# A new order for every engine in an attention and token-mixing kernel

## The chip, the core and the metric

The kernel runs on one core of a Trainium2 chip. A core has a matrix engine (TensorE, PE in the profile), a vector engine (VectorE, DVE), a scalar engine (ScalarE, ACT), a general engine (GpSimd, POOL) and a queue engine (SyncE, SP). Each takes its instructions strictly in the order in which the program gives them, and they wait for one another through semaphores. Loads and stores are DMA transfers, issued by SP, ACT or POOL and carried out by 16 DMA engines. The metric is the device time of one execution in microseconds.

## The reference

Inputs are q, k and v of shape (8 batches, 8 heads, 576 positions, 64), 32 packing queries p per head, and three weights. Two attentions stand one behind the other, then a token mixer:

```python
p_packed = sm_attn(p, k, v)            # 32 x 576 scores per head
out = sm_attn(q, p_packed, p_packed)   # 576 x 32 scores per head
x = out.transpose(0, 2, 1, 3).reshape(B, S, H * D)      # (8, 576, 512)
W_tok = scale * einsum('bsd,btd->bst', x @ w_q, x @ w_k)
y = maximum(einsum('bst,btd->bsd', W_tok, x), 0.0) @ w_out
```

The output is (8, 576, 512) in float32. The kernel computes in bf16 with float32 sums.

## The kernel before

All 8 batches are computed one after another with their steps interleaved. The work is written as some forty kinds of steps, each a small function; a string, ORDER (lines 12 to 59), lists every step of every batch, and a loop at the end of the function walks the string and issues the steps. So ORDER alone sets the sequence on every engine. `S1.5=0,1,6,7` is step S1 of batch 5 with PSUM banks 0, 1, 6 and 7; `GE.5@V` is step GE of batch 5 on VectorE (`@A` ScalarE, `@P` POOL). There are 8 PSUM banks, all in one tile, and a bank that is used again must first have been read out. Steps without an engine letter are TensorE's, or DMA issues: `LD.x` loads are issued by POOL unless a letter says otherwise, `ST` stores by SP unless it says POOL or ACT.

The chain of one batch b, in the order of the data:

- `LD.k`, `LD.v`, `LD.q` load the batch with a conversion to bf16 into one of four buffers each. For batches 0 and 7 q comes in halves: `LD.r0` and `LD.r7` (half 0), `LD.q0` and `LD.q7` (half 1). `LD.g0` is half 1 of the first k; its half 0 comes by `LD.H`, float32, and is converted by HC on ScalarE. `LD.E0`, `LD.E1`, `LD.P0` to `LD.P3` load p, `LD.W0`, `LD.W1` and `LD.O` the weights.
- KT (L246) transposes k in 32x32 blocks on VectorE; S1 (L282 for batches 0 and 1, L292 for the others) makes the scores of p; X1 (L300, L303) is their exponential on ScalarE; TE transposes it (VectorE, from batch 2 on). For the first two batches p is laid out by EC, EX and PB, for the others by PX.
- PV (L325) multiplies with v; RC and PP (L329, L333) normalise; PT transposes the packed result, which is key and value of the second attention.
- QV transposes q; S2 (L383) makes the scores of q; X2 (L388) is their exponential; RS, RR and AM (L404, L409, L415) sum the rows, take the reciprocal and multiply. For batch 5, HA on POOL (L398) first adds the halves of the rows. AM's chunk 3 covers four of the five row tiles (128x1024), chunk 2 the fifth (128x256); batches 0, 1 and 7 use chunks 0, 1 (128x512) and 2.
- AT (L424, L429) transposes the weights on TensorE and AE copies them out of PSUM; QK, QKE and QD make the mixer's small weights and a second copy of them; WKQ (L451, L456) and WE make the mixer's projections; GM, GE, Y, YE, MX (L502), MR (L508) mix the tokens; RL, RLF and RLR (L513, L515) are the ReLU.
- OT (L550) multiplies by w_out: five steps per batch, of four 128x512 matmuls each; the fifth (`OT.1.4` and so on) serves two batches at once. OH (L587) are two half-width ones at the very end. OE, OEF and OEH copy the results out of PSUM (L131 on ScalarE, L135 on VectorE); ST, STF and STH store them.

`SET` steps are memsets and other small preparations (`SET.v1` fills the ones in a v buffer, L213; `SET.idb` casts an identity). `WARM.n` issues n matmuls (L622) whose result nobody reads; they fill TensorE's time. `HOLD.v7` is a tiny DMA on SP that reads the last v buffer, so that the stores listed behind it on SP are not issued before v7 has landed. POOL's loads are also bounded by their semaphores: eight of them serve in turn, and a ninth load waits for the first to land.

The loop that does it:

```python
for item in ORDER.split():
    name, _, bk = item.partition("=")
    name, _, eng = name.partition("@")
    ...
    elif f[0] == "WARM":
        ps = bank(int(bk), [512])
        for _ in range(int(f[1])):
            nc.tensor.matmul(ps, warm[:, 0:P], warm, start=True, stop=True)
    else:
        bk = [int(z) for z in bk.split(",")] if bk else None
        steps[f[0]](*[int(z) for z in f[1:]], eng,
```

Of the kernel before, what the change touches and what calls it, by code (L numbers as in the profile page):

```python
# [33 lines left out]
MX.2.0=0,1 PV.4.0=6,7 PV.4.1 RS.3.4@V RL.2.1@A OE.1.0@A RL.2.0@A OT.1.2=4,5 RC.4@V RR.3.4@V PP.4.1@V
PP.4.0@V LD.q5 AM.3.3@P OT.1.3 PT.4@V QV.4.2@V OE.1.1@A QK.4=7 MR.2=0,1 QK.3=6 AM.3.2@V AT.3.3=2
AT.3.2=3 S2.4.2=4,5 AE.3.3@V RLR.2@A QKE.3@A AE.3.2@A QKE.4@A X2.4.2@A S2.4.3=0,1 KT.5.2@V X2.4.3@A
QD.3@P WKQ.3.0=2,3 WKQ.3.2 WKQ.3.1 OT.2.2=4,5 WE.3.2@A RS.4.4@V S1.5=0,1,6,7 GM.3=2 X1.5.1@A OT.2.3
KT.6.2@V GE.3@A X1.5.0@A Y.3=6,7 OT.2.0=2,3 YE.3@A OE.2.1@A MX.3.0=6,7 MX.3.1=0,1 RR.4.4@V TE.5.1@V
TE.5.0@V RL.3.0@A OT.2.1 RL.3.1@V PV.5.0=4,5 OE.2.0@A LD.v6 LD.q6 AM.4.3@P LD.k7 LD.v7 QD.4@P
AM.4.2@V PV.5.1 S1.6=0,1,6,7 RC.5@V AT.4.3=2 AT.4.2=3 PP.5.0@V PP.5.1@V OT.3.0=4,5 X1.6.0@A X1.6.1@A  # L40
AE.4.3@V AE.4.2@V PT.5@V TE.6.0@V QV.5.2@V TE.6.1@V WKQ.4.0=6,7 WKQ.4.1 WKQ.4.2 OT.3.1 QK.5=2
WE.4.2@A OE.3.0@A GM.4=3 GE.4@V MR.3=6,7 S2.5.3=0,1 Y.4=4,5 RLR.3@V YE.4@V QKE.5@A X2.5.3@A
PV.6.0=2,3 LD.r7 LD.q7 ST.0.0@P ST.0.1@P QD.5@P PV.6.1 S2.5.2=4,5 RC.6@V MX.4.1=0,1 PP.6.1@V PP.6.0@V X2.5.2@A
MX.4.0=6,7 OT.3.2=4,5 RL.4.1@A HA.5@P OT.3.3 RL.4.0@A PT.6@V QV.6.2@V RS.5.4@V S2.6.2=0,1 X2.6.2@A
S2.6.3=2,3 MR.4=6,7 RR.5.4@V QK.6=0 X2.6.3@A RLR.4@V OT.3.4=1 AM.5.3@P AM.5.2@P KT.7.2@V OE.3.1@A
# [609 lines left out]
```

## Time and profile before

| | us |
|---|---|
| median of 3 runs | 106.33 (106.15 to 106.53) |
| the profiled execution | 106.69 |
| its span, first to last instruction | 104.9 |
| TensorE busy | 93.5 (89%) |
| VectorE busy | 75.1 (72%) |
| ScalarE busy | 65.8 (63%) |
| POOL busy | 45.9 (44%) |

The span begins with the first instruction of the program. A slice of the page's second part is a fortieth of the span, and a digit is the busy share in tenths. A line of a timeline gives the start, the duration, the engine, the line of the program, the operation, output and input, shapes and count, and in brackets the idle time before it with what ended it. TensorE's matmuls overlap, so the price of a step is read from its start to the next start. A line of DMA issues gives the size and the median time from issue to landing. A line of windows gives the stretch, its length, the busy time with the instructions in brackets, the clock share, the share of the DMA engines and GB/s.

### The profile page before, as it was taken

To read this page: it belongs to the slowest core of one execution; us is meant where nothing else is said; L and a number is where in the kernel's file an instruction comes from. 1 tells how busy PE (TensorE), PEld (TensorE's weight loads), DVE (VectorE), ACT (ScalarE), POOL (GpSimd) and SP (SyncE) were. 2 spreads that over 40 slices of the span, in tenths; PEclk is the share of its full clock that TensorE was granted. 3 is DMA by queue.
4 is the path that set the end of the run, shared out by engine and by line. 5 is a ranking of instruction groups with operands and counts; after the bars stand their busy time and mean duration, and the time that the engine had idled before them with its cause. 6 is when DMAs were issued, how large, how long until landed. Compare 5 with 4: busy or idle time off the path is not lost.

```text
span 104.9 us, 3598 instructions
## 1 busy us (share of the span) xinstructions
PE 93.5 (89%) x1528; PEld 52.2 (50%) x1550; DVE 75.1 (72%) x151; ACT 65.8 (63%) x108; POOL 45.9 (44%) x74
## 2 busy tenths in 40 slices
PE   0994998998998999989999999999999999999930
PEld 0341654564645654655547436565466653743510
DVE  5056069969798889588598988969995989768000
ACT  5140404234657867879989897598996885556640
POOL 5977343554783226222054559635847029000000
PEclk9999999999999999999999999999999999999999
DMA  3999999999999999999999999999999999978693
GB/s 86 239 153 194 211 202 204 211 209 210 206 213 213 204 207 216 210 210 206 212 212 207 216 205 208 213 210 211 212 337 399 409 414 408 391 273 355 243 337 121
DMA packets 14079, 25.16 MB, mean 240 GB/s; under 512 B 2160, under 2 KB 7024, under 8 KB 14064
## 3 DMA queue, kind: packets, MB, share of 16 engines
q0 software_dynamic: 10160, 15.83, 81.4%
q1 hardware_dynamic: 3488, 8.91, 22.0%
q8 instruction: 12, 0.20, 0.7%
q10 hardware_dynamic: 416, 0.20, 0.7%
q14 instruction: 3, 0.02, 0.1%
HBM read 30.28 MB, written 9.44 MB: 379 GB/s over the span
## 4 chain that ended last, share of the span: by engine, by line
PE 67%; DVE 9%; DMA 7%; ACT 5%; issue 4%; POOL 3%; DVEq 0%; POOLq 0%; ACTq 0%
PE ps L550 26%; PE ps L622 8%; DMA k_sb<-in_k_dram 7%; PE ps L325 6%; PE ps L383 5%; PE ps L502 4%; PE ps L429 3%; PE ps L456 3%; PE ps L451 3%; POOL a L415 3%; DVE rs L404 3%; PE ps L282 2%; PE ps L477 2%; PE ps L346 2%; PE ps L292 2%
## 5 line engine op out<-in xcount | busy, mean ns | idle before, releaser
L550 PE MATMUL ps<-wout,relu 128*128 128x512 bf16 x113 | 29.4, 380 | 0.7 <-issue 0.2
L622 PE MATMUL ps<-o 128*128 128x512 bf16 x73 | 20.3, 410 | 2.9 <-DVE o L138 2.4
L415 POOL TENSOR_TENSOR a<-e,rr 128x1024 bf16<-128x1024 f32 (+2 forms) x10 | 12.5, 1263 | 17.3 <-DVE rr L409 17.3
L131 ACT ACTIVATE o<-ps 128x1024 f32<-128x1024 f32 (+2 forms) x18 | 15.2, 857 | 4.7 <-PE ps L550 4.7
L550 PEld LDWEIGHTS <-relu 128*128 128x128 bf16 x124 | 10.8, 98 | 11.9 <-issue 2.2
L388 ACT ACTIVATE e<-ps 128x256 f32<-128x256 f32 (+2 forms) x19 | 11.1, 620 | 7.7 <-PE ps L383 7.5
L622 PEld LDWEIGHTS <-o 128*128 128x128 bf16 x82 | 7.6, 103 | 11.4 <-issue 2.9
L180 POOL DMA_DIRECT2D v_sb<-in_v_dram x16 | 10.1, 637 | 6.9 <-PE ps L508 2.1
L404 DVE TENSOR_REDUCE rs<-e 128x16 f32<-128x512 f32 (+2 forms) x13 | 10.9, 842 | 2.0 <-ACT e L388 1.8
L246 DVE STREAM_TRANSPOSE kT<-k_sb 128x1152 uint32<-128x1152 uint32 (+1 forms) x9 | 11.0, 1228 | 1.6 <-DMA k_sb<-in_k_dram 1.6
L513 ACT ACTIVATE relu<-ps 128x1024 bf16<-128x1024 f32 (+1 forms) x12 | 11.1, 955 | 0.6 <-PE ps L508 0.6
L246 DVE STREAM_TRANSPOSE qT<-q_sb 128x1152 uint32<-128x1152 uint32 (+1 forms) x10 | 11.1, 1106 | 0.0
L131 ACT ACTIVATE wkq<-ps 128x448 bf16<-128x448 f32 (+1 forms) x10 | 7.1, 732 | 2.9 <-PE ps L456 2.2
L303 ACT ACTIVATE e1T<-ps 128x576 bf16<-128x576 f32 x12 | 7.4, 650 | 1.6 <-PE ps L292 1.6
L325 PE MATMUL ps<-v_sb,e 64*64 64x192 bf16 x288 | 7.5, 245 | 0.0
L383 PEld LDWEIGHTS <-qT 64*128 64x128 bf16 x320 | 5.5, 94 | 2.8 <-DVE qT L246 1.6
L300 ACT ACTIVATE e<-ps 128x1152 bf16<-128x1152 f32 x2 | 2.3, 1130 | 7.2 <-PE ps L282 7.2
L456 PE MATMUL ps<-aT,pqk 128*128 128x256 bf16 (+1 forms) x48 | 6.8, 246 | 0.0
L325 PEld LDWEIGHTS <-e 64*64 64x64 bf16 x288 | 5.8, 107 | 1.9 <-ACT e L300 1.0
L383 PE MATMUL ps<-ppT,qT 64*128 64x64 bf16 x320 | 6.4, 190 | 0.3 <-DVE qT L246 0.2
L515 DVE TENSOR_SCALAR relu<-ps 128x1024 bf16<-128x1024 f32 (+1 forms) x6 | 6.0, 1034 | 0.5 <-PE ps L502 0.5
L189 POOL DMA_DIRECT2D q_sb<-in_q_dram x6 | 4.3, 720 | 4.8 <-DMA q_sb<-in_q_dram 2.8
(78 smaller groups left out, 143.0 us busy)
## 6 DMA issues: line engine op xcount, KB each, us to landing
out_dram<-o SPq DMA_DIRECT2D x11, 512.0 KB, 5.9
v_sb<-in_v_dram POOLq DMA_DIRECT2D x16, 288.0 KB, 11.2
k_sb<-in_k_dram POOLq DMA_DIRECT2D x7, 576.0 KB, 11.9
q_sb<-in_q_dram POOLq DMA_DIRECT2D x6, 576.0 KB, 14.3
out_dram<-o SPq DMA_DIRECT2D x5, 256.0 KB, 2.4
q_sb<-in_q_dram POOLq DMA_DIRECT2D x4, 288.0 KB, 11.1
out_dram<-o POOLq DMA_DIRECT2D x2, 512.0 KB, 14.1
out_dram<-orem SPq DMA_DIRECT2D x4, 256.0 KB, 5.8
```

The source lines that it names most:

```text
L131: nc.scalar.activation(o, i, COPY)
L180: nc.gpsimd.dma_start(v_bufs[b % NL][halves(i), 0:7:2], src)
L246: nc.vector.transpose(o, i)
L325: nc.tensor.matmul(T["pv", b][halves(cc), i], lhsT, rhs, start=n == 0, stop=n == R - 1, skip_group_check=True)
L383: nc.tensor.matmul(ps[:, y, t - t0, i], lhsT, rhs, start=e == 0, stop=e == 1)
L388: nc.scalar.activation(e2[:, t0:t1].rearrange("a t (i y n) -> a y (t i) n", i=2, y=2), T["s2", b, c].rearrange("a y t i n -> a y (t i) n") ...
L404: nc.vector.tensor_reduce(rs[:, t0 * H:t1 * H], src, axis=AX, op=ADD)
L415: e.tensor_tensor(a2[:, t0:t1].rearrange("a t i (u l) -> a (t i u) l", l=L), e2v(b, c), T["rr", b][:, t0 * H:t1 * H].to_broadcast((P, (t1 ...
L456: nc.tensor.matmul(o, pqk[:, i, Dl:], aT[:, i, c0:c1], start=i == 0, stop=i == 1)
L513: nc.scalar.activation(o, i, RELU)
L550: nc.tensor.matmul(ps, lhsT, wout[:, j, :], start=j == 0, stop=j == NJ - 1)
L622: nc.tensor.matmul(ps, warm[:, 0:P], warm, start=True, stop=True)
```

## The change

Only ORDER is different; no step's function is touched, and the same steps are issued, apart from the warm-up matmuls (15 groups with 82 matmuls before, 12 groups with 72 after). All engines get another sequence, the PSUM banks are dealt out anew, and 55 steps change engine. Among them:

- memsets v1 and v2 from VectorE to POOL; POOL's loads in another sequence at the start (P1 and P3 early, v0 after q0, k1 later), with QV.0.1 and KT.0.0 ahead of KT.0.1 on VectorE, and PX ahead of QV.1.2 and PT.1
- AM.4.3, AM.5.3, AM.6.3 and AM.7.1 from POOL to VectorE; AM.1.0, AM.2.2, AM.2.3 and AM.4.2 in the main the other way
- QD from POOL to ScalarE (batches 0 and 2) or VectorE (3 to 6); OE.3.0 and OE.6.0 from ScalarE to VectorE; several AE, RL, RLR, GE, YE and WE between the two
- LD.r7 behind HA.5, and LD.q7 behind the store ST.0.0 and behind AM.5.2 on POOL; ST.0.1 later on POOL
- another sequence of the last matmuls, copies and stores

The diff, cut:

```diff
 ORDER = """
-LD.H@S LD.E0@A LD.E1@S SET.v0@V SET.pz0@V SET.aT0@V SET.warm@V SET.tab@A EC@A HC@A EX@V SET.v1@V SET.idf@V PB.0.2@V
-LD.g0 LD.v0 LD.q0 SET.v3@P SET.mask@P PB.0.0@P PB.0.3@V KT.0.1@V KT.0.0@V PB.0.1@V
-WARM.21=1 S1.0=0,2,4 X1.0.0@A WARM.5=7 PV.0.0=0,1 PV.0.1 RC.0@V QV.0.1@V PP.0.0@V PP.0.1@V LD.r0
-LD.k1 LD.W1 LD.W0 SET.aff@P SET.idb@V PT.0@V QV.0.0@V WARM.11=2 S2.0.2=0,1 S2.0.0=2,3 LD.v1 LD.P3
-LD.q1 LD.P2 SET.v2@V KT.1.2@V LD.P1 LD.P0 S2.0.1=4,5 X2.0.1@A X2.0.0@A X2.0.2@A RS.0.1@V SET.aT1@V
...
-PV.6.0=2,3 LD.r7 LD.q7 ST.0.0@P ST.0.1@P QD.5@P PV.6.1 S2.5.2=4,5 RC.6@V MX.4.1=0,1 PP.6.1@V PP.6.0@V X2.5.2@A
-MX.4.0=6,7 OT.3.2=4,5 RL.4.1@A HA.5@P OT.3.3 RL.4.0@A PT.6@V QV.6.2@V RS.5.4@V S2.6.2=0,1 X2.6.2@A
-S2.6.3=2,3 MR.4=6,7 RR.5.4@V QK.6=0 X2.6.3@A RLR.4@V OT.3.4=1 AM.5.3@P AM.5.2@P KT.7.2@V OE.3.1@A
-OT.4.0=2,3 RS.6.4@V S1.7=4,5,6,7 OEF.3.4@A QKE.6@A AT.5.3=1 AT.5.2=0 OT.4.1 AE.5.3@V HOLD.v7
-X1.7.1@A X1.7.0@A AE.5.2@V RR.6.4@V OE.4.0@A WKQ.5.0=4,5 QD.6@P AM.6.3@P AM.6.2@P WKQ.5.2 WKQ.5.1
...
+SET.pz0@V SET.v0@V LD.E0@A LD.H@S LD.E1@S LD.g0 SET.warm@V SET.tab@A SET.idf@V EC@A EX@V PB.0.2@V PB.0.1@V
+SET.aT1@V SET.v2@P LD.P1 LD.q0 HC@A KT.0.0@V LD.P3 PB.0.0@P PB.0.3@V QV.0.1@V KT.0.1@V WARM.31=0 S1.0=0,1,2
+X1.0.0@A LD.v0 WARM.5=3 PV.0.0=4,5 PV.0.1 LD.r0 RC.0@V SET.mask@P PP.0.0@V PP.0.1@V PT.0@V QV.0.0@V LD.W1
+WARM.9=3 S2.0.1=6,7 SET.aff@P SET.idb@V LD.k1 KT.1.2@V S2.0.2=0,1 X2.0.1@A SET.v3@P S2.0.0=2,3 X2.0.0@A
+SET.v1@P LD.W0 RS.0.0@V SET.aT0@V RR.0.0@V LD.P2 LD.v1 AM.0.0@V RS.0.1@V WARM.8=4 S1.1=4,5,6 X1.1.0@A X2.0.2@A
+RS.0.2@V RR.0.2@V AM.0.2@V LD.q1 WARM.5=7 PV.1.0=2,3 QK.0=7 PV.1.1 RC.1@V PP.1.1@V AT.0.0=6 PP.1.0@V LD.P0
+QKE.0@A RR.0.1@V AM.0.1@V PX@V QV.1.2@V AT.0.2=7 AE.0.0@A QD.0@A WARM.2=4 WKQ.0.0=4,5 WARM.1=0 AT.0.1=6
...
+GE.4@V S2.5.2=6,7 X2.5.2@A TE.6.1@V S2.5.3=4,5 TE.6.0@V OE.3.0@V Y.4=0,1 YE.4@V PV.6.0=6,7 PV.6.1 RC.6@V
+PP.6.0@V LD.v7 QK.5=2 X2.5.3@A HA.5@P PP.6.1@V MX.4.1=4,5 MX.4.0=0,1 QKE.5@A QD.5@V RL.4.1@A PT.6@V MR.3=2,3
+LD.r7 RLR.3@A RL.4.0@A OT.3.2=6,7 RS.5.4@V OT.3.3 OE.3.1@A QV.6.2@V OT.3.4=4 MR.4=2,3 ST.0.0@P RLR.4@A
+S2.6.3=0,1 OEF.3.4@A S2.6.2=6,7 RR.5.4@V AM.5.2@P AM.5.3@V OT.4.0=2,3 X2.6.2@A HOLD.v7 AT.5.3=5 KT.7.2@V
+AT.5.2=4 AE.5.2@V LD.q7 ST.3.4 ST.1.4 X2.6.3@A AE.5.3@A ST.2.1 RS.6.4@V RR.6.4@V AM.6.2@P OT.4.1 AM.6.3@V
+OE.4.0@A ST.1.1 S1.7=6,7,0,1 X1.7.0@A TE.7.0@V WKQ.5.0=4,5 WKQ.5.2 WKQ.5.1 WE.5.2@A OT.4.2=2,3 OT.4.3 X1.7.1@A
+TE.7.1@V AT.6.2=6 AE.6.2@A GM.5=7 GE.5@A OE.4.1@A AT.6.3=4 QK.6=5 ST.3.1 QV.7.0@V ST.4.0 Y.5=0,1 AE.6.3@V
+PV.7.0=6,7 PV.7.1 QV.7.1@V YE.5@A MR.5=2,3 RC.7@V QKE.6@A QD.6@V RLR.5@A MX.5.1=0,1 MX.5.0=4,5 PP.7.0@V
+WKQ.6.0=2,3 WKQ.6.1 WKQ.6.2 RL.5.1@A PP.7.1@V OT.5.4=6 PT.7@V S2.7.0=0,1 RL.5.0@A WE.6.2@V S2.7.1=4,5
...
+YE.6@V MX.6.1=6,7 ST.2.0 MX.6.0=2,3 ST.4.1 ST.5.4 AM.7.1@V AT.7.1=4 AM.7.0@P AE.7.2@V QD.7@P AE.7.1@A RL.6.0@A
+AT.7.0=5 OT.5.1 AE.7.0@V ST.3.0 RL.6.1@V WKQ.7.0=4,5 WKQ.7.1 WKQ.7.2 WE.7.0@A OT.6.0=2,3 WE.7.1@V OE.5.0@V
+ST.5.1 ST.5.0 GM.7=6 GE.7@A OT.6.1 OE.6.0@V Y.7=4,5 MR.6=6,7 OT.6.2=0,1 RLR.6@A YE.7@A MR.7=6,7 ST.6.0 RLR.7@V
+MX.7.0=4,5 MX.7.1=2,3 RLF.7.0.0@V RLF.7.0.1@V RLF.7.1.0@V OEF.6.2@A STF.6.2 OT.6.3 OEF.6.3@A STF.6.3
+RLF.7.1.1@A OT.7.4=0 OEF.7.4@V ST.7.4 OT.7.2=6 OEF.7.2@V STF.7.2 OT.7.0=7 OEF.7.0@A OT.7.1=4 OEF.7.1@A
+OH.7.1=5 STF.7.0 STF.7.1 OEH.7.1@V OH.7.0=1 OEH.7.0@A STH.7.1@A STH.7.0
```

## The prediction

> **What bounds the kernel now.** I read the page's slices first, then TensorE's timeline, then the landings of the loads, then VectorE in the stretch where it is fullest.
>
> The slices, 2.62 us each:
>
> ```profile
> PE   0994998998998999989999999999999999999930
> DVE  5056069969798889588598988969995989768000
> DMA  3999999999999999999999999999999999978693
> ```
>
> TensorE is full from about 30 us to 100 us, and the 16 DMA engines are full from 2.6 us to about 92 us. Two resources are nearly used up. VectorE stands at 8 and 9 in slices 21 to 34.
>
> TensorE's timeline, cut to the places the sum uses:
>
> ```profile
> 2.44 6.51 PE L622 MATMUL ps<-o 128*128 128x512 bf16 x21 [2.44 <-DVE o L138]
> 10.35 1.24 PE L282 MATMUL ps<-o,kT 128*64 128x128 bf16 x36 [1.41 <-DVE o L135]
> ...
> 30.67 0.48 PE L292 MATMUL ps<-kT,pT 32*32 32x288 bf16 x32
> ...
> 58.78 0.48 PE L292 MATMUL ps<-kT,pT 32*32 32x288 bf16 x32
> 59.20 0.47 PE L477 MATMUL ps<-wkq,a 128*128 128x64 bf16 x10
> 59.50 1.03 PE L550 MATMUL ps<-wout,relu 128*128 128x512 bf16 x4
> 60.45 0.25 PE L487 MATMUL ps<-pp,g 64*64 64x128 bf16 x4
> ...
> 75.58 0.49 PE L292 MATMUL ps<-kT,pT 32*32 32x288 bf16 x32
> ...
> 84.35 0.78 PE L383 MATMUL ps<-ppT,qT 64*128 64x64 bf16 x40
> ```
>
> The L292 rows are S1.2, S1.5 and S1.7; the last row is S2.7. From start to start each step has a price: S1 0.42, GM 0.30, OT 0.95 (59.50 to 60.45; two in a row 1.78), and likewise WKQ 0.80, PV 0.87, S2 0.70, MX 0.55, AT 0.52, QK 0.36, Y 0.20, MR 0.13. With these, the steps between S1.5 and S1.7 sum to 16.77 against 16.80 measured, and those from S1.7 to S2.7 to 8.78 against 8.77. So TensorE does not wait there; its own work is the bound.
>
> The loads (time to landing; 288 KB each half of q7, 576 KB k7) and VectorE's busy time from KT.5.2 to PT.7:
>
> ```profile
> k_sb<-in_k_dram POOLq DMA_DIRECT2D x1, 576.0 KB, 10.2
> v_sb<-in_v_dram POOLq DMA_DIRECT2D x2, 288.0 KB, 11.7
> q_sb<-in_q_dram POOLq DMA_DIRECT2D x2, 288.0 KB, 13.0
> ```
> ```profile
> 56.80:83.20 26.40, 23.14 (x45) 1.00 1.12 256
> ```
>
> k7 is issued at 63.23 and lands at 73.4; KT.7.2 follows at 73.93 and S1.7 at 75.58. v7 lands at 76.6, r7 at 78.0, q7 (issued 66.00, 13.4) at 79.4. Loads arrive one behind the other, 1.4 us per 288 KB, with 7 to 18 us of queue ahead of each. Both orders load the same bytes before k7, so k7 lands at 73.4 in both unless the queue runs dry.
>
> **The change, part by part.**
>
> Front. QV.0.1 moves ahead of KT.0.1 on VectorE and needs q0. POOL now issues P1 between g0 and q0, and v0 later. By landings (g0 8.6; 0.3 for 64 KB of P, from 24.5, 24.8, 25.1; 1.4 for q0) q0 lands at 10.3 instead of 12.8. QV.0.1 (0.75) and KT.0.1 (0.75) then end at 11.85 and S1.0 starts at 12.1, against 10.35: +1.75. Its 31 warm-ups end near 11.0. Afterwards QV.0.1 (0.75) and the cast idb (0.21) are gone from between RC.0 and QV.0.0, so S2.0 is late by 0.8 to 1.0 only. k1 lands 1.3 later (P1, P3 and W1 are ahead), S1.1 slips by 0.7, PV.1 by 0.6. PX now sits ahead of QV.1.2 and PT.1 and waits for P0 (25.1): S2.1 at about 27.8 against 26.45, while WKQ.0 and GM.0 are done before it. QK.1, Y.0 and S1.2 follow at 29.7 against 30.67. Next v2 decides, loaded behind q2 now: it lands at 33.5 (q2's time before, 22.12 + 11.4), PV.2 runs at 33.7 against 34.51. The delay is covered by warm-ups; without that cover it costs up to 1.75.
>
> Warm-ups: 82 become 72, at 0.216 each when hot (128x512). Behind S1.2 there are 4 instead of 12, 1.7 us less of TensorE work. Between there and S1.5 most of this goes into waiting for loads: S2.3 needs q3 (47.3) plus QV 1.35, S2.4 needs QV.4.2 and PT.4, S1.5 needs k5 (39.49 + 17.1 = 56.6) plus KT.5.2 1.37, so 58.0 against 58.78. What stays: S1.5 0.8 earlier, with OT.2.3 done, MR.2 and QK.4 not.
>
> Small memsets: v1 and v2 move to POOL, 0.64 each by the v3 row against 0.54 on VectorE. They lie beside the load-bound front: nothing. They need only precede PV.1 and PV.2.
>
> Division of the copies. By rows VectorE takes on 2.8 us over the whole (80.8 to 83.6), ScalarE 1.0, and POOL is relieved of 4.1. Between KT.5.2 and PT.7 VectorE's list goes from 25.0 to 27.1: AM.4.3, AM.5.3, AM.6.3 (1.18 each), three QD and OE.3.0 (1.21) come in, against RL.3.1 (1.2), AM.4.2, two RLR, AE.5.3 and others. In measured terms 23.1 busy becomes 25.2 of the same 26.4; the idle 3.3 that absorbed waits shrinks to about 1.2. QD has no VectorE row; bounds are the 32x256 copy (0.22) and POOL's own (0.29); I take 0.22, its kind of instruction. QD on ScalarE (0, 2) takes 0.28 as the 128x128 casts. AE of 128x1024 on ScalarE lies between 0.60 (half the size) and 1.02 (f32): 1.0. WE.6.2 on VectorE lies between 0.62 (half) and 1.21: 1.1.
>
> What this does to TensorE, walked from S1.5 at 58.0 by the prices above: the steps up to S1.7 sum to 17.44 (AT.5 and OT.4.1 now stand ahead of S1.7, QK.6 behind it). MX.3 waits 0.15 for YE.3, which queues behind AM.4.3 and TE.5.1; PV.6 0.25 for v6 and TE.6.0; MX.4 0.4 for YE.4, queued behind OE.3.0. KT.7.2 is queued behind AM.5.3 and starts near 74.7, not at 73.9. S1.7 at 76.4: 0.8 late, with 1.1 us less work ahead of it to S2.7 (7.67 instead of 8.78). That gives 84.1. ScalarE (X2.6, AE.5.3, OE.4.0 ahead of X1.7.0) just serves it.
>
> q7. LD.q7 stood at 66.0 on POOL; now it is behind HA.5, LD.r7, the 512 KB store ST.0.0 and AM.5.2. HA.5 ends near 70.5, RR.5.4 (behind QV.6.2) near 73.4, AM.5.2 (0.61) near 74.1. Then q7's bytes stand behind those of r7 and ST.0.0: 80.7, ST.0.0's own landing before (66.69 + 14.0), is the lower bound; 82.3, that of ST.0.1 beside SP's stores (68.13 + 14.2), the upper. I take 81.0, the nearer in bytes. QV.7.1 then runs to 82.0 ahead of RC.7, QD.6, PP.7, PT.7, which end at 83.2; S2.7 asks for it at 84.1, so 0.9 us cover it. WKQ.6 waits for QD.6 and is just in time.
>
> AM pairs. RR.4.4, RR.5.4 and RR.6.4 now release an AM on VectorE and one on POOL at once. No row before shows two of these side by side: AM.3.3 on POOL (53.59, 1.90) ran beside transposes at their usual 1.34. The bounds are 0 and 0.6 (AM.6.2 waiting out most of AM.6.3, AT.6.2 being next on TensorE); a gain is excluded, since each has its lone price in the sum. I take 0.3, having no nearer row.
> The Trainium skill (SBUF — State Buffer, "SBUF: two separate sides") says that a VectorE operation with two SBUF inputs and a GpSimd operation share one pair of ports, and that whichever starts first holds it throughout. No row of this trace shows it. By that rule the second AM waits out the first; the sum would have 0.6 here instead of 0.3.
>
> Tail. OE.6.0, YE.6, RLF.7.1.0, OEF.7.2 and 7.4 change engine. Walked from S2.7, TensorE's steps take 16.65 to the last OH against 16.3 (84.35 to 100.65): AM.7.1 follows RS.7.1 and YE.6 on VectorE, and WKQ.7 and OT.6.0 wait for AE.7.0 and RL.6.1. After the last matmul, one 0.38 copy and one store, as before. +0.35.
>
> Sum: S2.7 -0.2, AM pair +0.3, tail +0.35: +0.45 on a span of 104.9, so 105.35. The profiled execution took 106.69 in all, 0.36 above the median 106.33; the median stands 1.43 above the span, so **106.8 us**.
>
> **The rivals.** Second, the lead is kept: VectorE's waits turn out smaller than the three I add, S1.7 runs when k7 allows (73.4 + 0.2 + 1.4 = 75.1, or 0.5 before now) with 1.1 less to do: -1.6 at best, with the tail's +0.35 -1.2, halfway 105.5. For it: the fewer warm-ups, S1.5 early. Against: VectorE's 25.2 of 26.4. It decides if KT.7.2 starts before 74.3. Third, q7 arrives after 82, or the AM pairs cost their whole: past 82 every tenth delays PT.7, and past PT.7 at 84.1 also S2.7; at 83 with the pair at 0.6 it is +1.6, 107.9. For it: AM.5.2 stands ahead of LD.q7. Fourth, the steps cancel: 106.3, the change being spent beside the loads.
>
> **How the numbers follow.** Forecast 0.40, lead kept 0.33, late q7 or pairs 0.15, cancelled 0.12. Faster 0.33, within 0.3% (0.32 us, about what measurement of this kernel can tell) 0.13, slower 0.54, from the first (mostly over 0.3%) and the third. The range runs from the better half of the second (105.2) to a little past the third (108.4); the forecast's own is 106.4 to 107.4, by the bounds of pair (0 to 0.6) and q7.
>
> **What would show it.** S1.0 near 12; S1.5 near 58.0; KT.7.2 after 74.5 behind AM.5.3; S1.7 near 76.4 with AT.5 and OT.4.1 before it; q7 landing near 81; VectorE with hardly a gap from 57 to 83; AM on both engines at once, each longer than alone or not; the last matmul near 101.1. I am wrong if S1.5 is already late (then front or queue), or if S1.7 comes at 75 (then VectorE was no bound).

## The result and the profile after

The changed kernel takes 110.41 us (median of 6 runs, 109.37 to 111.26) against 106.39 of the kernel before on the same chip: 1.035 times the time, 95% interval 1.030 to 1.040. It is slower by 4.0 us in the medians and by 3.7 in the ratio, outside the forecast's range. The profiled execution took 110.31 with a span of 108.5. Some executions of this program, in either order, run longer at a lower granted clock; ratios are formed without them, and for two of the experiments too few others were left for a ratio.

The slices of the page of after, 2.71 us each:

```profile
PE   1999999998939979998796999989999899799940
DVE  5075077788898768987699999979999769888610
DMA  3999999999999999999999946999999999999973
GB/s 85 273 180 198 185 201 198 213 212 210 207 214 175 180 187 201 211 205 218 209 213 204 214 86 79 204 211 206 190 248 297 412 411 402 404 402 356 363 287 125
```

TensorE has dents where it had none (slices 12, 15, 20 and 22), and the DMA engines, which were full to 92 us before, fall to 4 and 6 in the 24th and 25th slice: 86 and 79 GB/s in place of some 210.

TensorE's timeline, cut to the same steps and to the four places where it stands longest between S1.2 and S1.7:

```profile
29.08 0.53 PE L288 MATMUL ps<-kT,pT 32*32 32x288 bf16 x32
...
31.89 0.23 PE L420 MATMUL ps<-idb,a 128*128 128x64 bf16 x2 [1.83 <-DVE a L411]
...
40.44 1.04 PE L546 MATMUL ps<-wout,rem 128*128 128x512 bf16 x4 [0.59 <-DVE rem L511]
...
50.90 0.25 PE L483 MATMUL ps<-pp,g 64*64 64x128 bf16 x3
52.19 0.24 PE L483 MATMUL ps<-pp,g 64*64 64x128 bf16 x1 [1.04 <-issue]
...
58.99 0.78 PE L379 MATMUL ps<-ppT,qT 64*128 64x64 bf16 x40 [0.87 <-DVE ppT L242]
61.46 0.48 PE L288 MATMUL ps<-kT,pT 32*32 32x288 bf16 x32
...
79.07 0.48 PE L288 MATMUL ps<-kT,pT 32*32 32x288 bf16 x32
...
87.32 0.78 PE L379 MATMUL ps<-ppT,qT 64*128 64x64 bf16 x40
```

The L288 rows are S1.2, S1.5 and S1.7, the L379 rows S2.4 and S2.7. S1.2 is 1.6 earlier than before, S1.5 2.7 later. Between them lie stops: at AT.1.2 (from 30.05), at OT.1.4, in the middle of Y.2, and ahead of S2.4. The stops of TensorE longer than 0.14 us behind 30 us, measured between its records with the weight loads counted as work, sum to 0.8 before and to 5.6 after: 1.83 at AT.1.2, 0.59 OT.1.4, 1.04 Y.2, 0.68 S2.4, 0.37 PV.6, 0.44 in two places near S2.7, 0.63 at AT.7.1. That is 4.8 more, against 5.3 by which the way from S1.2 to the last matmul grew (69.98 to 75.24). The eight warm-ups that are gone from this way (1.7) are made up in part by matmuls at half clock in one slice (PV.2 took 1.65 instead of 0.94). That slice is not the loss: the profiled executions of e1, e2 and e3 below have a granted clock of 1.00 and take 109.28 to 110.39.

| start, us | before | after | forecast |
|---|---|---|---|
| S1.0 | 10.35 | 10.47 | 12.1 |
| S1.2 | 30.67 | 29.08 | 29.7 |
| S1.5 | 58.78 | 61.46 | 58.0 |
| S1.7 | 75.58 | 79.07 | 76.4 |
| S2.7 | 84.35 | 87.32 | 84.1 |
| end of the last matmul | 100.65 | 104.32 | 101.1 |

The stop at AT.1.2 waits for AM.1.2, the end of a chain on VectorE (sums, reciprocals and multiplication of batch 1). The kernel before has the same step at the same time, with almost no wait:

```profile
31.90 0.23 PE L424 MATMUL ps<-idb,a 128*128 128x64 bf16 x2
```

So TensorE's lead of 1.6 at S1.2 ended here: what it had done ahead, it then waited for VectorE. S1.3 stands at 39.36 after and at 39.25 before. The end of the chain, on VectorE and POOL in the kernel after:

```profile
30.90 0.93 DVE L411 TENSOR_TENSOR a<-e,rr 128x256 bf16<-128x256 f32 x1
```
```profile
30.50 1.04 POOL L411 TENSOR_TENSOR a<-e,rr 128x512 bf16<-128x512 f32 x1 [9.57 <-ACT e1T L299]
```

AM.1.2, 0.42 in the kernel before, took 0.93 beside AM.1.0 on POOL.

The stop ahead of S2.4 waits for PT.4. What stands ahead of PT.4 is the pair AM.3.2 (VectorE, 128x256) and AM.3.3 (POOL, 128x1024). VectorE's and POOL's timelines there:

```profile
55.19 2.01 DVE L411 TENSOR_TENSOR a<-e,rr 128x256 bf16<-128x256 f32 x1
```
```profile
55.01 1.91 POOL L411 TENSOR_TENSOR a<-e,rr 128x1024 bf16<-128x1024 f32 x1 [6.76 <-DVE rec L325]
...
63.44 1.22 POOL L411 TENSOR_TENSOR a<-e,rr 128x256 bf16<-128x256 f32 x1 [5.80 <-ACT e1T L299]
64.61 1.28 POOL L176 DMA_DIRECT2D v_sb<-in_v_dram  x2
```

AM.3.2 takes 0.40 alone; here it ends 0.3 behind POOL's operation. The last two rows are AM.4.2 and, behind it, LD.v6: POOL stood 5.8 us for AM.4.2's turn and issued v6 at 64.6, where the kernel before issued it at 57.2. That is the hole in the DMA row. VectorE's window from 57 to 83 us is as full as forecast (25.2):

```profile
56.80:83.20 26.40, 25.36 (x42) 1.00 1.02 189
```

### The profile page after: what moved, and what is told of

Read it like the earlier page. It is cut to its first block, busy times and chain, and to the rows that moved or that the text cites. A ratio compares the mean times of both kernels' runs of the same rounds, so it can differ in the third digit from the quotient of the medians.

```text
span 108.5 us, 3589 instructions
## 1 busy us (share of the span) xinstructions
PE 95.1 (88%) x1540; PEld 53.3 (49%) x1540; DVE 81.5 (75%) x152; ACT 66.3 (61%) x112; POOL 44.7 (41%) x69
## 4 chain that ended last, share of the span: by engine, by line
PE 41%; DMA 21%; DVE 17%; POOL 9%; issue 5%; ACT 2%; SPq 0%; POOLq 0%; DVEq 0%; ACTq 0%
PE ps L546 17%; DMA k_sb<-in_k_dram 11%; DMA q_sb<-in_q_dram 6%; DVE rs L400 4%; PE ps L321 4%; DVE a L411 4%; DMA o<-in_p_dram 3%; PE ps L379 3%; PE ps L452 3%; DVE qT L242 2%; PE ps L425 2%; POOL v_sb L176 2%; PE ps L447 2%; PE ps L288 2%; PE ps L498 2%
## 5 line engine op out<-in xcount | busy, mean ns | idle before, releaser
L546 PE MATMUL ps<-wout,relu 128*128 128x512 bf16 x124 | 30.5, 380 | 0.0
L411 POOL TENSOR_TENSOR a<-e,rr 128x256 bf16<-128x256 f32 (+2 forms) x9 | 11.4, 1276 | 39.7 <-ACT e1T L299 15.4
L618 PE MATMUL ps<-o 128*128 128x512 bf16 x72 | 19.4, 410 | 2.3 <-DVE o L134 2.3
L127 ACT ACTIVATE o<-ps 128x1024 f32<-128x1024 f32 (+2 forms) x15 | 13.0, 867 | 7.5 <-PE ps L546 7.1
L618 PEld LDWEIGHTS <-o 128*128 128x128 bf16 x72 | 6.7, 103 | 9.8 <-DVE o L134 2.3
L411 DVE TENSOR_TENSOR a<-e,rr 128x512 bf16<-128x512 f32 (+2 forms) x10 | 10.5, 1048 | 0.2
L127 ACT ACTIVATE aT<-ps 128x512 bf16<-128x512 bf16 (+2 forms) x12 | 6.3, 534 | 5.6 <-PE ps L425 4.8
L321 PE MATMUL ps<-v_sb,e 64*64 64x192 bf16 x288 | 9.1, 260 | 0.7 <-issue 0.4
L321 PEld LDWEIGHTS <-e 64*64 64x64 bf16 x288 | 6.9, 114 | 3.0 <-issue 1.2
L379 PE MATMUL ps<-ppT,qT 64*128 64x64 bf16 x320 | 6.4, 190 | 1.1 <-DVE ppT L242 0.9
L379 PEld LDWEIGHTS <-qT 64*128 64x128 bf16 x320 | 5.7, 94 | 2.5 <-DVE qT L242 1.3
L127 ACT ACTIVATE wkq<-ps 128x448 bf16<-128x448 f32 (+1 forms) x8 | 5.8, 731 | 1.7 <-PE ps L447 1.3
```

Source lines behind the costliest of these rows:

```text
L127: nc.scalar.activation(o, i, COPY)
L321: nc.tensor.matmul(T["pv", b][halves(cc), i], lhsT, rhs, start=n == 0, stop=n == R - 1, skip_group_check=True)
L379: nc.tensor.matmul(ps[:, y, t - t0, i], lhsT, rhs, start=e == 0, stop=e == 1)
L411: e.tensor_tensor(a2[:, t0:t1].rearrange("a t i (u l) -> a (t i u) l", l=L), e2v(b, c), T["rr", b][:, t0 * H:t1 * H].to_broadcast((P, (t1 ...
L546: nc.tensor.matmul(ps, lhsT, wout[:, j, :], start=j == 0, stop=j == NJ - 1)
```

## The experiments

Four causes were in question: the late loads on POOL, the AM pairs that hold each other up, the stops with the releaser "issue" (the profile shows nothing that TensorE waits for), and the fuller VectorE. In the diffs a line is a cut of ORDER.

### One cause at a time, taken out of the kernel after

**e1** issues v6 and q6 ahead of the waiting AM.4.2:

```diff
-AM.4.2@P S1.5=2,3,6,7 ... TE.5.1@V LD.v6 OT.2.1 ... LD.q6 RL.3.0@A
+LD.v6 LD.q6 AM.4.2@P S1.5=2,3,6,7 ... TE.5.1@V OT.2.1 ... RL.3.0@A
```

> Changed kernel, with LD.v6 and LD.q6 moved ahead of AM.4.2 on POOL, nothing else. In the changed kernel LD.v6 was issued at 64.6 us, after POOL had waited for RR.4.4 and for the lock, the load queue ran dry around 64 us and k7 landed at 76.6 instead of 73.4. Theory Q (the dry queue is the cause): v6 is issued near 57.7, k7 lands near 73.7, S1.7 comes 2 to 3 us earlier, time about 108. Theory V (VectorE is late before that, S1.5 at 61.5 already): k7 lands near 73.7 as well, but S1.5 stays near 61.5 and S1.7 near 78.9, and only q7's wait near 84 goes: 109.7 to 110.3.

Measured: 109.8 against 106.14, ratio 1.034 (1.026 to 1.043). k7 landed at 73.44 and q7 at 82.27 instead of 76.60 and 84.68, S1.5 came at 60.8, S1.7 at 78.4. The queue no longer runs dry and nothing is gained that a run can tell: TensorE is late at S1.5 already, before any of these loads is needed, as theory V had it.

**e2** puts AM.3.2 ahead of AM.3.3 on POOL, so that no pair stands there:

```diff
-AM.3.2@V
+AM.3.2@P
```

> Changed kernel, with AM.3.2 on POOL ahead of AM.3.3 instead of on VectorE beside it. In the changed kernel AM.3.2 took 2.01 us on VectorE where its form takes 0.41. Theory L (the two engines lock each other out): PP.4.1, QV.4.2 and PT.4 come 1.6 to 2.0 us earlier, S2.4 near 57.2 instead of 59.0, S1.5 near 59.8, and the load of v6 is issued as much earlier; time about 108.6 to 109. Theory Q: v6 is issued earlier by the same 1.6, so a similar gain, but with S1.7 set by k7. If the 2.01 was the operation's own (the line held up by something else), S2.4 stays at 59 and the time at 110.4.

Measured: 109.65, ratio 1.0345 (1.027 to 1.042). The stop ahead of S2.4 is gone, S1.5 comes at 60.8. Yet nothing is gained: the stop in Y.2 grew to 1.39, and PV.6 waits 0.63, here for v6 and at another place of the stream than in the kernel after; all stops together are 6.1 instead of 5.6.

**e3** takes the 128x256 halves of batches 4, 5 and 6 to VectorE, so that they no longer run on POOL beside VectorE's halves:

```diff
-AM.4.2@P ... AM.5.2@P AM.5.3@V ... AM.6.2@P
+AM.4.2@V ... AM.5.2@V AM.5.3@V ... AM.6.2@V
```

> Changed kernel, with AM.4.2, AM.5.2 and AM.6.2 on VectorE, just ahead of or behind AM.b.3 there, so that no AM runs on POOL in these batches. Theory L: each pair costs VectorE 0.41 more and spares POOL's wait of about 1; AM.4.3, 5.3, 6.3 keep 1.2 each; v6 is issued near 57.7, q7 near 74.5; S1.5 stays near 61.5. S1.7 comes only 0 to 0.5 earlier, S2.7 0.5 to 1: time 109.3 to 110. Theory Q: k7 near 73.7 and S1.7 2 to 3 us earlier: about 108.

Measured: 110.42, ratio 1.039 (1.031 to 1.047): nothing gained. On POOL beside VectorE's half they had taken 1.22, 1.56 and 1.58 against 0.61 alone, but TensorE did not wait for them longer than 0.2.

**e4** is e1, e2 and e3 together.

> Changed kernel, with the three edits together: AM.3.2 on POOL, AM.4.2, 5.2, 6.2 on VectorE, LD.v6 and LD.q6 early. Theory L with Q: S1.5 near 59.8, k7 near 73.7, S1.7 near 77, S2.7 near 85: time 107.7 to 108.5; what is still above the kernel before (106.4) is then VectorE's added work and the front. Theory V alone (too much VectorE work, no lock): no more than 0.5 gained.

Measured: 109.98, ratio 1.036 (1.026 to 1.046). S1.5 at 60.5, S1.7 at 78.5. The sum of these three causes is not the loss. Nor is the time a plain sum of stops: those of e4's profile are 4.0 in place of 5.6, and no gain can be told.

### The same causes, put into the kernel before

**f2** moves AM.3.2 ahead of PT.4 in the kernel before, where it stands beside AM.3.3:

```diff
-PT.4@V QV.4.2@V ... QK.3=6 AM.3.2@V AT.3.3=2
+AM.3.2@V PT.4@V QV.4.2@V ... QK.3=6 AT.3.3=2
```

> Kernel before, with one step moved: AM.3.2 on VectorE ahead of PT.4 instead of behind QV.4.2, so that it runs beside AM.3.3 on POOL. Theory L: it takes about 1.8 to 2.0 us instead of 0.39, POOL's AM.3.3 keeps 1.9, and PT.4, QV.4.2 and S2.4 come about 1.6 later than their work asks; time up by 0.4 to 1.2. Rival (the 2.01 belongs to the changed kernel's surroundings): 0.4, time unchanged.

Measured: 107.79 against 106.28, ratio 1.014 (1.007 to 1.022). VectorE, POOL and TensorE in f2:

```profile
53.32 2.00 DVE L415 TENSOR_TENSOR a<-e,rr 128x256 bf16<-128x256 f32 x1
```
```profile
53.13 1.90 POOL L415 TENSOR_TENSOR a<-e,rr 128x1024 bf16<-128x1024 f32 x1 [4.55 <-DVE rr L409]
```
```profile
55.59 0.41 PE L346 MATMUL ps<-wqk,ppT 64*64 64x128 bf16 x8 [1.50 <-DVE ppT L246]
```

POOL started first and kept its 1.90; VectorE's operation, 0.40 alone, ended 0.3 behind it, PT.4 came late and TensorE stood 1.50. This is what the Trainium skill (SBUF — State Buffer, "SBUF: two separate sides") states of the shared pair of ports: whichever starts first holds it for the whole instruction. The pair alone is worth 1.4%.

**f3** holds v6 and q6 behind AM.4.3 in the kernel before:

```diff
-LD.v6 LD.q6 AM.4.3@P
+AM.4.3@P LD.v6 LD.q6
```

> Kernel before, with LD.v6 and LD.q6 behind AM.4.3 on POOL, so that they are issued near 63.3 instead of 57.2 and 58.4. Theory Q: the load queue runs dry near 65, v6, q6 and k7 land 1 to 2 us later, S1.7 follows k7 and the time rises by 1 to 2. Rival (a gap of the queue is hidden by TensorE's backlog): under 0.5.

Measured: 108.66, ratio 1.023 (1.017 to 1.029). Its page shows the same hole in the DMA row, and TensorE's waits a new one that goes back to POOL:

```profile
DMA  2999999999999999999999949999999999999793
```
```profile
PE ps L456 <- POOL pqk L133: 1.4, 1, 1.4
```

QD.4 now has the issue of v6, q6, k7 and v7 ahead of it on POOL in one row, ends at 67.0 and holds WKQ.4 up by 1.4; k7 is late too, and KT.7.2 holds S1.7 up by 0.5. So the edit costs 2.3% where nothing else is late, the larger part of it through QD.4 and only some 0.5 us through the late k7; in the kernel after, where TensorE is late already, issuing the loads early gains nothing that can be told (e1).

### The stops with the releaser "issue"

In the kernel after and in e1 to e4 TensorE stops in Y.2 at the same place of its stream, its 1470th weight load or matmul, and in all of them but e2 again at the 2236th (e2's wait in PV.6, for v6, is at the 2179th). The difference, 766, is three times 256 but for two. The trace's DMA packets have one of 16 KB on the instruction queue 2.2 to 2.6 us before each of these stops ends (in the kernel after at 49.73 and 69.63, for stops that end at 52.19 and 72.05). **f1** takes ten warm-ups away, so that every later instruction stands 20 places further forward:

```diff
-WARM.31=0 S1.0=0,1,2
+WARM.21=0 S1.0=0,1,2
```

> Changed kernel with 21 instead of 31 warm-up matmuls ahead of S1.0, where TensorE waits anyway; all instructions behind them move up by 20 places in TensorE's stream. In all five traces of the changed order TensorE stands still inside Y.2 at the same place of the stream (after 1470 weight loads and matmuls) for 0.66 to 1.39 us, and again inside PV.6 766 instructions later, each time 2.1 to 2.6 us after a 16 KB transfer of the instruction queue began. Theory F (the stall is the fetch of the next 256 instructions): the stall leaves Y.2 and comes 20 instructions later, after OT.1.1 has begun, so it shrinks to 0.3 or less; S1.5 about 0.7 earlier; time 109.3 to 110. Rival (a semaphore of Y.2): the stall stays in Y.2 and the time at 110.2.

Measured: 109.75 against 106.28, ratio 1.032 (1.026 to 1.038). Y.2 has no stop any more; that of PV.6 has moved a few steps on in the order, into the middle of QK.5, and is longer. It is the 2224th instruction recorded in f1, where 19 records are missing:

```profile
70.52 0.30 PE L342 MATMUL ps<-wqk,ppT 64*64 64x128 bf16 x4
72.34 0.30 PE L342 MATMUL ps<-wqk,ppT 64*64 64x128 bf16 x4 [1.52 <-issue]
```

No data, bank or engine decides where TensorE stops, but the count of instructions. By these figures it stops where a block of 256 has been used up before the next one is there. The time of the 256 instructions that end at each stop, without the stop itself: 4.5 us at Y.2 in after (stop 1.04), 4.3 at PV.6 (0.37), 4.6 there in h3 below (0.46). The fastest block of the kernel before takes 5.3 to 5.5 (22 of its records are missing), and none of its stops is of this kind. There is no fixed bound: i2 below stops 0.93 behind a block of 4.9, h4 0.87 behind one of 5.5, while one of 5.2 in i1 passes without a stop. The packet itself begins 2.4 to 4.3 us after TensorE has passed the edge before (46.37 and 49.73 in after, 70.15 and 74.42 in h4); why it varies is not shown. The Trainium skill (Runtime: NRT & Kernel Launch, "Instruction fetch mechanics") has blocks of 16 KiB or 256 instructions, and calls the crossing mostly hidden; the size agrees, the hiding fails here.

**f4** closes what the traces so far named: e4 and f1, OT.1.4 a place later, AM.7.0 on VectorE, and r7 and q7 issued earlier.

```diff
-WARM.31=0 ... OT.1.4=4 OEF.1.4@A X1.3.1@A RS.2.4@V OT.0.2=2,3 OT.0.3
+WARM.21=0 ... X1.3.1@A RS.2.4@V OT.0.2=2,3 OT.1.4=4 OEF.1.4@A OT.0.3
-HA.5@P ... LD.r7 ... LD.q7 ... AM.7.0@P
+LD.r7 LD.q7 HA.5@P ... AM.7.0@V
```

> Changed kernel with every gap of TensorE attacked at once that its trace shows behind S1.3: AM.3.2 on POOL; AM.4.2, 5.2, 6.2 and 7.0 on VectorE; OT.1.4 behind OT.0.2 (it waited 0.6 for RLR.1); 21 warm-ups; LD.v6, LD.q6, LD.r7 and LD.q7 early. Theory S (no single cause; the loss is the sum of TensorE's gaps, 6.0 us in the changed kernel against 2.7 before): gaps fall to about 3 and the time to 107.5 to 108.3. Rival W (too much work on VectorE, so that a closed gap opens elsewhere): gaps stay above 4.5 and the time above 109.

Measured: 110.21, ratio 1.028 (1.017 to 1.040). Theory S missed; the rival's numbers hold (stops of 5.0), but not by its reason: AT.1.2 still waits 1.81, and the stop of QK.5, which has nothing to do with VectorE, is there with 1.38, since f4 has f1's count.

### The division between the engines, and the order

**g1** is the order after with the 55 moved steps back on their old engines, **g2** the order before with the 55 on their new ones. In cut:

```diff
-QD.0@A ... AM.4.3@V ... OE.3.0@V
+QD.0@P ... AM.4.3@P ... OE.3.0@A
```

> The order and the banks after, but each of the 55 steps that changed engine back on the engine it had before. Theory W (VectorE was given too much): VectorE's busy time falls from 81.5 towards 75 us and with it S1.5 and S1.7 come earlier; a time of 107 to 108. Theory O (it is the order of the steps, whatever engine does them): within 0.7 of the kernel after, 109.4 to 110.8, S1.5 still at 60.5 or later, and the pair AM.3.2 and AM.3.3, which stands on VectorE and POOL in both kernels, still with the 128x256 half at about 2.0.

> The kernel before with its own order and banks, but each of the 55 steps on the engine that it has after. Theory W: VectorE's list grows by the same rows and the time rises by 1.5 to 3, to 108 to 109.3. Theory O: 106 to 107, S1.5 near 58.8 and S1.7 near 76.

Measured: g1 128.27 against 106.44, ratio 1.204 (1.198 to 1.210); g2 123.32, ratio 1.153 (1.143 to 1.163). Both theories missed widely. POOL's timeline in g2 has the largest piece:

```profile
34.36 0.73 POOL L179 DMA_DIRECT2D k_sb<-in_k_dram  x1
46.16 0.61 POOL L411 TENSOR_TENSOR a<-e,rr 128x256 bf16<-128x256 f32 x1 [11.07 <-DVE rr L405]
46.73 0.77 POOL L185 DMA_DIRECT2D q_sb<-in_q_dram  x1
```

AM.2.2, put on POOL at the place where it stood in VectorE's list, waits 11 us for its reciprocal with LD.q3, LD.v4, LD.q4 and LD.k5 behind it. **g3** and **g4** exchange only the 38 steps between VectorE and ScalarE and leave POOL's list alone:

```diff
-AE.0.0@A ... RL.3.1@A ... OE.3.0@V
+AE.0.0@V ... RL.3.1@V ... OE.3.0@A
```

> The kernel before, with only the 38 steps that moved between VectorE and ScalarE on the engine they have after; POOL's list stays as before. Theory P (in the exchange of all engines the time was lost by waiting work put ahead of loads on POOL): the 15% shrink to under 3%, 106 to 109.5, and no slice of the DMA row under 6. Theory D (an order fits only its own division between VectorE and ScalarE): 112 or more.

> The kernel after, with the 38 steps between VectorE and ScalarE back on the engine they had before; POOL's list stays as after. Theory P: 109 to 112, near the kernel after, against 128 with POOL's steps exchanged too. Theory D: 115 or more.

Measured: g3 114.96 against 106.56, ratio 1.079 (1.076 to 1.082); g4 120.5, ratio 1.129 (1.124 to 1.134). POOL's list was about half of g2's loss, and 7.5 of the 17% by which g1 is above the kernel after; the rest belongs to the other two engines. Where it goes shows in g4, in TensorE's waits and VectorE's timeline:

```profile
PE ps L447 <- DVE aT L131: 3.4, 1, 3.4
```
```profile
25.11 1.03 DVE L242 STREAM_TRANSPOSE pT<-o 128x512 uint32<-128x512 uint32 x1
26.00 1.33 DVE L242 STREAM_TRANSPOSE qT<-q_sb 128x1152 uint32<-128x1152 uint32 x1
27.25 0.39 DVE L131 COPY aT<-ps 128x512 bf16<-128x512 bf16 x1
```

AE.0.0 (27.25) queues on VectorE behind PX and QV.1.2, and WKQ.0 waits 3.4 us for it, while ScalarE, which does it in the kernel after, stands idle from 23.8 to 29.0. Neither division is better in itself: each order is written for its own. With that, what the division alone costs can't be read off by an exchange, and VectorE's extra 6.4 us of busy time (75.1 to 81.5) stays unpriced.

### Which stretch costs

**h3** takes all that stands ahead of S1.5 in the kernel before, in its order, and then what is left in the order after. **h4** is the reverse, with MR.2 on banks 2 and 3.

> All steps of the kernel before that stand ahead of S1.5, in its order, banks and engines; then what is left, in the order, banks and engines after. If the loss arises ahead of S1.5 (there 61.46 against 58.78 in the profiles): S1.5 near 58.8 and a time of 106.5 to 107.5, the rest of the order after costing at most the 1.0 that its stretch from S1.5 to the end is longer (42.9 against 41.9). If the stretch behind S1.5 is the cause (loads held on POOL, VectorE full from 57 to 83): S1.5 near 58.8 too, but 108.5 or more.

> The reverse: the order, banks and engines after for all that stands ahead of S1.5, then what is left of the kernel before (MR.2 on banks 2 and 3). If the loss arises ahead of S1.5: S1.5 at 61 or later and 108.5 to 109.5. If it arises behind: the late S1.5 is made up in part, LD.v6 and LD.q6 being issued early again, and the time is 106.5 to 107.5.

Measured: h3 108.32, ratio 1.015 (1.010 to 1.021), S1.5 at 59.18, S1.7 at 77.38. This is at the edge between the two readings: more than half of the 3.5% goes when the first part goes, and 1.5% stay behind S1.5, 0.68 us of them a wait of OT.2.0 for OE.2.1 at the seam, which the kernel after does not have. h4 took 113.67 (110.82 to 114.42, no ratio): its seam, a wait of 1.54 ahead of S1.5, and a stop of 1.71 in Y.2 hide what was asked. **h7** is h3 with the loads early:

```diff
-RR.4.4@V AM.4.2@P S1.5=2,3,6,7 ... LD.v6 ... LD.q6
+RR.4.4@V LD.v6 LD.q6 AM.4.2@P S1.5=2,3,6,7 ...
```

> The order before up to S1.5 and the order after behind it, with LD.v6 and LD.q6 ahead of AM.4.2 on POOL. If the dry load queue is what the part behind S1.5 costs: q7 lands 2 earlier, S1.7 near 76.4, and the time falls from 108.3 to about 107.0. If TensorE and VectorE are late there on their own: within 0.5 of 108.3, with S1.7 still at 77 or later.

Measured: 109.64 (107.56 to 114.92, no ratio). In its profile the DMA row has no hole, and S1.7 comes 18.1 us behind S1.5, as in h3 (18.2). The edit moved the landings little: k7 lands at 72.86 instead of 73.61 in h3 and q7 at 81.45 instead of 81.67, where the kernel after has 76.60 and 84.68. In h3 k7 was about as early as in the kernel before (73.43), so late loads are not what the part behind S1.5 costs there.

### Four stops at once

**i1** sets out to take four stops out of the kernel after together: e1's and e2's, AM.1.0 on VectorE (it ran on POOL beside AM.1.2, which took 0.93 there instead of 0.42, and AT.1.2 waits for AM.1.2), and 22 warm-ups, which move the blocks' edges by 44 instructions.

```diff
-WARM.31=0 ... WARM.9=3 ... WARM.8=4 ... AM.1.0@P ... AM.3.2@V ... AM.4.2@P ... LD.v6 ... LD.q6
+WARM.21=0 ... WARM.3=3 ... WARM.2=4 ... AM.1.0@V ... AM.3.2@P ... LD.v6 LD.q6 AM.4.2@P
```

> The kernel after with four of its stops taken away: LD.v6 and LD.q6 ahead of AM.4.2; AM.3.2 on POOL ahead of AM.3.3; AM.1.0 on VectorE, so that it does not run beside AM.1.2; 22 warm-ups fewer ahead of S1.1, so that the edge of an instruction block falls 44 instructions further on in the stream. Theory S (the loss is the sum of the named stops): gaps of TensorE behind 30 us fall from 5.6 to under 3 and the time to 107 to 108.2. Theory M (a stop taken away comes back as another, since the engines stand in a tight chain): the gaps stay above 4.5 and the time within 0.7 of 109.8.

Measured: 108.66 against 106.56, ratio 1.021 (1.016 to 1.026), between the two theories, and so are the stops with 4.0. Those at AT.1 did not go: AM.1.2 is short again, but AT.1.0 now waits for AM.1.0, and the three steps wait 1.00, 0.22 and 0.53, together 1.75 instead of 1.83. S1.3 comes at 38.92, no earlier than in e1 and e2 (38.66, 38.86). S1.5 comes at 58.85, as early as in the kernel before (58.78). From S1.3 to S1.5 it takes 19.9 us; after took 22.1, of which its stops at Y.2 and S2.4 are 1.72 and the shrinking of that at OT.1.4 0.40: 22.1 - 2.1 = 20.0, in spite of a new stop of 0.40 ahead of AT.3.3. So between S1.3 and S1.5 the stops are the loss. Behind it a new one opened, at instruction 2236 once more, now ahead of OT.3.2:

```profile
69.95 0.23 PE L504 MATMUL ps<-wkq,y 64*128 64x64 bf16 x4
71.26 1.90 PE L546 MATMUL ps<-wout,relu 128*128 128x512 bf16 x8 [1.07 <-DVE ppT L242]
```

The profile puts it down to PT.6, whose result OT.3.2 doesn't read; the banks that OT.3.2 needs were read out at 70.1. The 256 instructions ahead had taken 4.4 us. **i2** takes ten more warm-ups away, to move the edges once more, and **i3** also puts AM.7.0 on VectorE behind AM.7.1:

```diff
-WARM.21=0 ... WARM.5=3 ... WARM.5=7 ... AM.7.0@P
+WARM.19=0 ... WARM.1=3 ... WARM.1=7 ... AM.7.0@V
```

> i1 with 10 warm-ups fewer ahead of S1.1 (32 fewer than the kernel after), so that every edge of 256 instructions falls 20 instructions further on in the stream, where by i1's times each block has lasted 4.9 us or more. Theory F (TensorE stops for its next block where 256 instructions are used up in less than about 4.6 us): no stop at 2236, no other of more than 0.3 with the releaser issue, S1.7 near 76, time 107.3 to 108.0. Theory M (the stop comes back in another form): within 0.4 of i1's 108.7.

> i2 with AM.7.0 on VectorE behind AM.7.1, so that AM.7.1 has no neighbour on POOL. Theory L (the two lock each other out): AM.7.1 takes about 0.65 in place of 1.4, the stop ahead of AT.7.1 (0.63) goes, the time is 0.3 to 0.6 under i2's, 106.8 to 107.5. If the pair costs nothing: the same as i2.

Measured: i2 109.0 over eleven runs against 106.29, ratio 1.013 (1.006 to 1.020) from four of them; i3 109.84 over five, ratio 1.010 (1.000 to 1.021) from two. In i2 the same two steps stand without a stop:

```profile
70.39 0.23 PE L504 MATMUL ps<-wkq,y 64*128 64x64 bf16 x4
70.56 1.90 PE L546 MATMUL ps<-wout,relu 128*128 128x512 bf16 x7
```

S1.7 comes at 76.68, S2.7 at 84.73. In i3 S1.7 is at 75.99 and S2.7 at 84.04 (75.58 and 84.35 in the kernel before). But the stop has only moved again. Behind S2.7 it stands ahead of GM.6, 0.93 in i2 and 1.17 in i3:

```profile
86.44 0.47 PE L473 MATMUL ps<-wkq,a 128*128 128x64 bf16 x10 [0.93 <-issue]
```
```profile
86.00 0.47 PE L473 MATMUL ps<-wkq,a 128*128 128x64 bf16 x10 [1.17 <-issue]
```

It is the 2732nd instruction recorded in i2. By the rows that lack matmuls, 16 of its 19 missing records lie ahead, which makes it the 2748th, twice 256 behind 2236; a 16 KB packet began 2.3 us before the stop's end. Theory F's condition, no other stop of this kind above 0.3, failed. AM.7.1 on VectorE beside AM.7.0 on POOL took 1.42 in i2; in i3 VectorE does both, one behind the other, in 1.37:

```profile
89.05 1.37 DVE L411 TENSOR_TENSOR a<-e,rr 128x512 bf16<-128x512 f32 x2
```

The stop at AT.7.1 goes in i3, but the gain over i2 is inside the intervals. i3's span also ends 6.1 us behind its last matmul, where the kernel before has 4.3; why is not shown. With 32 warm-ups fewer i2's runs spread from 107.07 to 111.35 at granted clocks of 0.91 to 1.00 (the two fastest had 0.98 and 1.00), and the page of i2 has the clock at half from the sixth slice to the ninth:

```profile
PEclk9999755557999999999999999999999999999999
```

No version beat the kernel before.

## Why the prediction was wrong

**The walk's prices were right, its waits were not.** From S1.5 to S1.7 the forecast had 17.44 of work and three waits of 0.8 together, and put S1.7 18.4 behind (the terms sum to 18.24). The kernel after took 17.6, of which 0.37 is a stop of another kind: none of the three waits came. i1 took 17.1 without its own stop. From S1.7 to S2.7 the forecast had 7.67, i1 took 7.75, after 8.26 with two stops of 0.44. From S2.7 on it had 17.0 with the pairs, and after took 17.0, with a stop of 0.63 in it. So the order after does the work behind S1.5 in about the time that was summed for it. The loss of 3.2 us against the forecast's end (104.32 against 101.1) stands in the way to S1.5 (3.46 later than walked), and is made in the main of stops that the sum did not have. That the forecast had "slower" is luck: its 0.45 came from pairs behind S1.5 and the tail, and the loss came elsewhere.

**"S1.5 0.8 earlier": the step that failed.** It took the warm-ups' 1.7 us as room that only waits for loads would fill, named PT.4 as what S2.4 needs without pricing it, and set no wait for VectorE and no other stop ahead of S1.5. The lead was there (S1.2 at 29.08, forecast 29.7, and q0 at 8.93 instead of 10.3), and AT.1.2's wait of 1.83 for VectorE used it up before S1.3. From there to S1.5 three more stops came, 0.59 at OT.1.4, 1.04 in Y.2 and 0.68 ahead of S2.4, and S1.5 stood at 61.46 instead of 58.0. In i1, where the last two are gone and the first is 0.19, it stands at 58.85. The prediction's own sign of being wrong, S1.5 already late, had come.

**"AM pairs", 0.3 with bounds 0 and 0.6.** The rule of the Trainium skill that was set beside it holds, and the pairs it was set for are the wrong ones. Those of RR.4.4, RR.5.4 and RR.6.4 take 1.22 to 1.58 instead of 0.61 and cost nothing that e3 can tell. AM.3.2 beside AM.3.3 was not counted as a pair, because both kernels have these steps on these engines; what changed is its place on VectorE: it now starts beside AM.3.3, with QV.4.2 and PT.4 behind it. By f2 that is worth 1.4% in the kernel before. AM.1.2 and AM.7.1 were missed likewise.

**"k7 lands at 73.4 in both unless the queue runs dry."** It ran dry, and k7 landed at 76.6. The step looked at the bytes ahead of each load, not at LD.v6 behind AM.4.2 on POOL, though the order on POOL was in the diff. q7 landed at 84.68, past the bounds (80.7 to 82.3). In the kernel before held loads, with QD.4 behind them, cost 2.3%; here they were held while TensorE was late anyway, and e1 gained nothing.

**No term for the instruction blocks.** 1.41 us of after's stops are of this kind, and one of 0.9 to 1.5 came back at another step in f1, f4, i1, i2 and i3. Nothing in the profile of before shows one; its fastest block takes 5.3 to 5.5 us.

**VectorE as the bound** was right in its size between 57 and 83 us (25.36 against 25.2) and not in its part: the three waits did not come, and in i3 VectorE carries nearly the same list while S1.7 comes at 75.99, ahead of the 76.4 that were walked. Over the whole run the forecast gave VectorE 2.8 more; it was 6.4. Of this 2.9 are AM.1.2, AM.3.2 and AM.7.1, stretched beside POOL (0.42 to 0.93, 0.40 to 2.01, 0.69 to 1.42).

**The rivals.** The third (late q7 or dear pairs) named two of the mechanisms at 107.9 but put them behind S1.5. None had several of them in a row.

**What stays open.** e1, e2 and f1 gained next to nothing one by one, i1 1.4% of the time with e1, e2, more warm-ups taken away and AM.1.0 on VectorE. AM.1.0 was not run alone; by i1's stops at AT.1 (1.75 against 1.83) it gave next to nothing. No run took the wait at AT.1 away: i2 and i3 still have 1.53 there and 0.93 and 1.17 at GM.6, and what the lower clock of the front costs them is not separated. The 1.5% that h3 keeps behind S1.5 are explained only in part.

## What to carry to other kernels

When an order is rewritten, look for what now stands behind an unchanged step, not only at the steps that moved: put into a kernel that was otherwise on time, PT.4 behind AM.3.2 cost 1.4%, and v6 and q6 behind an AM on POOL, with QD.4 behind their issue, 2.3%. Work that one engine does ahead is no lead when the next step waits for another engine that comes no earlier, as AT.1.2 did. A stop taken out of a tight chain shows its worth only when its neighbours go too, so test causes in both directions, by taking them out of the slow kernel and by putting them into the fast one. Keep steps that wait from standing ahead of loads on the queue that issues them: in g2 one such wait was 11 us.

## What the runs showed of the hardware

- TensorE stops for its instructions. Stretches of 256 weight loads and matmuls that ran in 4.2 to 4.9 us, in h4 also one of 5.5, were followed by a stop of 0.2 to 1.7 us, which ended 2.2 to 2.6 us after a 16 KB packet on the instruction queue began. The place moves with the count of instructions: 10 warm-ups fewer moved it from PV.6 to QK.5, 22 fewer to OT.3.2, 32 fewer to GM.6. The profile calls it "issue", or names a releaser that the step does not need.
- A VectorE multiplication of two SBUF operands and one on POOL run one behind the other: 0.40 became 2.0 beside 1.9 on POOL, 0.61 on POOL became 1.2 to 1.6 beside 1.2 on VectorE. Two such on VectorE (1.37) took less time than one beside POOL's (1.42).
- With 32 of the 72 warm-up matmuls gone, the profiled execution of i2 had the granted clock at half for some 10 us in the front. It is not so in every execution: i2's had 0.91 to 1.00 in the mean, and the kernel after, with all 72, was at half clock in one slice.
